# Moving the routing and the scatter of a mixture-of-experts kernel into its recurrence loop, with expert tiles of 256 slots

## The chip, the cores and the metric

The kernel runs on one core of one Trainium2 chip. The metric is device time in microseconds (us). Three runs of the kernel before took 1472.67, 1475.0 and 1470.46 us; the median is 1472.67.

## What is computed

Inputs are x and f_logit (4 sequences of 5056 tokens, 256 wide), a lower bound for the gate, 8 expert embeddings, and two weight matrices for each expert (256x1024 and 1024x256).

```python
sig = 1.0 / (1.0 + np.exp(-f_logit))
f = lower_bound + (1.0 - lower_bound) * sig
i = 1.0 - f
for t in range(S):                      # per sequence, h starts at 0
    h = f[:, t] * h + i[:, t] * x[:, t]
    y[:, t] = h
```

All 4 x 5056 = 20224 rows of y then go through a router and one expert each:

```python
logits = (y / |y|) @ (emb / |emb|).T / tau
expert_idx = argmax(logits)             # one of 8
gate_w = softmax(logits)[expert_idx]
out = gate_w * (relu(y @ w1[expert_idx]) @ w2[expert_idx])
```

## The kernel before

Three stages follow one another, each with its own pools of memory. Every engine's program is written out by hand with its waits on semaphores; there is no scheduler. [...]

**Stage 1, the recurrence** (lines 186 to 400), 79 rounds of 256 tokens. SyncE loads x and f_logit. TensorE transposes both so that the 256 channels lie on partitions (`xT_ps`, `flT_ps`, lines 388 and 398). ScalarE makes the gate (tanh line 327, an affine line 331, and 1 - f line 337). VectorE multiplies (line 254) and runs the recurrence as a scan along the tokens (line 270). TensorE multiplies the result by a matrix that holds both the identity and the 8 expert embeddings (`merged_mms`, line 359); so `psum_rt` has the rows back in token order and, in its first 8 columns, their logits. VectorE copies both out, rows to `Yt_sb` for all 158 blocks of 128 tokens, and ScalarE sums the squares of each row (line 316). Beside this GpSimd fills the scratch table `XsScratch` with null rows (line 161, 166 transfers) and loads all weights as bf16 (lines 165 and 169).

**Stage 2, routing** (lines 460 to 563). All engines wait for stage 1 (`barrier_waits`). VectorE handles all 158 x 8 logits at once: the largest, a one-hot, the gate weight, and with two sets of matmuls (lines 582 and 587) the slot of each token in a table sorted by expert, where each expert's part is padded to a multiple of 128. Then GpSimd scatters the rows, one indirect transfer for each block of 128 tokens (line 558), 158 in all.

**Stage 3, the experts** (lines 565 to 765), 166 blocks of 128 slots. SyncE loads a block from the table (line 610) into one of four buffers `xsb`; from the fifth block on it first waits until the output of the block four places before has landed. TensorE transposes it (line 628), reads the number of its expert into a register (line 635), multiplies by w1 with tokens on the partitions of the result (line 642), transposes the hidden layer of the block before (line 659), and multiplies that of two blocks before by w2 (line 671). ScalarE applies relu (line 743), VectorE copies out both transposes (lines 701 and 708) and scales the output by the gate weight (line 721). GpSimd writes the rows to their places with an indirect transfer (line 750). The wait that closes the ring over the buffers is

```python
if sblk >= 4:
    sp.wait_ge(s_od[sblk % 2], 16 * (sblk // 2 - 1))
sp.dma_start(xsb[r4][:], Xs[sblk * P : (sblk + 1) * P, :])
```

## Time and profile before

| | |
|---|---|
| median of 3 runs | 1472.67 us (1470.46 to 1475.0) |
| profiled execution, its span from first to last instruction | 1469.9 us; no other time is given for it |
| mean granted TensorE clock | 0.820 of full speed |
| busy TensorE matmul / weight load / VectorE / ScalarE / GpSimd | 863.2 / 534.4 / 514.6 / 431.3 / 420.8 us |
| moved by DMA | 104.90 MB |
| share of the chain that ended last | TensorE 30%, DMA 25%, VectorE 12%, "issue" 12%, GpSimd 10%, ScalarE 8% |

The span is the time from the first to the last instruction of one profiled execution; the median of the runs lies 2.8 us above it. PE is TensorE, PEld its weight loads, DVE VectorE, ACT ScalarE, POOL GpSimd, SP SyncE. A wait is put down to what ended it. "Issue" is time in which an engine waited for nothing that the profile shows. [...]

### The profile page before, as it was taken

To read this page: it belongs to the slowest core of one execution; us is meant where nothing else is said; L and a number is where in the kernel's file an instruction comes from. 1 tells how busy PE (TensorE), PEld (TensorE's weight loads), DVE (VectorE), ACT (ScalarE), POOL (GpSimd) and SP (SyncE) were. 2 spreads that over 40 slices of the span, in tenths; PEclk is the share of its full clock that TensorE was granted. 3 is DMA by queue.
4 is the path that set the end of the run, shared out by engine and by line. 5 is a ranking of instruction groups with operands and counts; after the bars stand their busy time and mean duration, and the time that the engine had idled before them with its cause. 6 is when DMAs were issued, how large, how long until landed. Compare 5 with 4: busy or idle time off the path is not lost.

```text
span 1469.9 us, 18961 instructions
## 1 busy us (share of the span) xinstructions
PE 863.2 (59%) x4930; PEld 534.4 (36%) x4930; DVE 514.6 (35%) x1121; ACT 431.3 (29%) x805; POOL 420.8 (29%) x521
## 2 busy tenths in 40 slices
PE   5666676665100000377777777777777777777765
PEld 4555555554000000133434433333443433334433
DVE  4664566666700000123322233323323323233222
ACT  5775677775100000111112121111211111212111
POOL 9890000000077777312121111211111112111121
PEclk9998999999555555589888888988888888888887
DMA  7899844442011111111111111111111111111110
GB/s 214 235 231 235 178 130 129 128 124 64 4 53 53 52 49 53 37 41 39 39 43 39 38 38 41 40 37 43 37 41 39 36 39 41 35 42 39 39 41 20
DMA packets 96104, 104.90 MB, mean 71 GB/s; under 512 B 13828, under 2 KB 83727, under 8 KB 96016
## 3 DMA queue, kind: packets, MB, share of 16 engines
q1 hardware_dynamic: 67184, 52.67, 13.0%
q0 software_dynamic: 28832, 51.03, 12.3%
q8 instruction: 58, 0.95, 0.3%
q14 instruction: 30, 0.25, 0.1%
HBM read 69.42 MB, written 43.66 MB: 77 GB/s over the span
## 4 chain that ended last, share of the span: by engine, by line
PE 30%; DMA 25%; DVE 12%; issue 12%; POOL 10%; ACT 8%; POOLq 0%; DVEq 0%; SPq 0%; ACTq 0%
DMA out_dram<-osb,xsb 14%; DMA xsb<-XsScratch 11%; POOL XsScratch L558 10%; PE psum_h L642 10%; PE psum_o L671 8%; PE psum_rt L359 6%; PE hT_ps L659 4%; ACT fg L331 3%; DVE osb L721 3%; DVE Yf L270 3%; ACT junk L316 2%; PE ysT_ps L628 2%; DVE ixb L254 2%; ACT ig L337 2%; ACT th L327 2%
## 5 line engine op out<-in xcount | busy, mean ns | idle before, releaser
L743 ACT ACTIVATE h_sb<-psum_h 128x1024 bf16<-128x1024 f32 x166 | 169.8, 1023 | 913.9 <-PE psum_h L642 913.9
L750 POOL DMA_INDIRECT out_dram<-osb,xsb x166 | 163.2, 983 | 696.2 <-DVE osb L721 683.2
L628 PE MATMUL ysT_ps<-identb,xsb 128*128 128x128 bf16 x332 | 51.1, 240 | 408.9 <-DMA xsb<-XsScratch 408.4
L671 PE MATMUL psum_o<-w2b,hTt_sb 128*128 x1328 | 272.3, 312 | 0.8
L642 PE MATMUL psum_h<-w1b,ys_sb 128*128 x664 | 232.4, 485 | 60.5 <-DVE ys_sb L701 35.3
L359 PE MATMUL psum_rt<-RHS,Yf 128*128 128x264 f32 x632 | 165.1, 406 | 97.1 <-DVE R L286 93.7
L671 PEld LDWEIGHTS psum_o<-w2b,hTt_sb 128*128 128x128 bf16 x1328 | 149.6, 113 | 152.0 <-issue 68.8
L628 PEld LDWEIGHTS ysT_ps<-identb,xsb 128*128 128x128 bf16 x332 | 23.6, 103 | 438.4 <-issue 236.1
L558 POOL DMA_INDIRECT XsScratch<-Yt_sb,sloti x158 | 152.8, 967 | 88.2 <-issue 50.7
L717 DVE TENSOR_TENSOR gt<-xsb 128x1 f32<-128x1 bf16 x166 | 26.5, 160 | 412.8 <-PE psum_o L671 412.8
L701 DVE COPY ys_sb<-ysT_ps 128x256 bf16<-128x256 bf16 x166 | 47.8, 288 | 346.2 <-PE ysT_ps L628 345.9
L359 PEld LDWEIGHTS psum_rt<-RHS,Yf 128*128 128x128 f32 x632 | 118.1, 197 | 130.0 <-DVE Yf L270 97.2
L642 PEld LDWEIGHTS psum_h<-w1b,ys_sb 128*128 128x128 bf16 x664 | 71.5, 108 | 157.7 <-issue 113.5
L708 DVE COPY hTt_sb<-hT_ps 128x1024 bf16<-128x1024 bf16 x166 | 114.4, 689 | 36.6 <-PE hT_ps L659 36.1
L659 PE MATMUL hT_ps<-identb,h_sb 128*128 128x128 bf16 x1328 | 121.6, 245 | 2.5 <-ACT h_sb L743 2.0
L270 DVE TENSOR_TENSOR_SCAN Yf<-fg,Yf,ixb 128x256 f32<-128x256 f32 (+2 forms) x156 | 107.4, 729 | 2.8
L659 PEld LDWEIGHTS hT_ps<-identb,h_sb 128*128 128x128 bf16 x1328 | 96.9, 111 | 4.8 <-ACT h_sb L743 4.7
L254 DVE TENSOR_TENSOR ixb<-ig,xT_ps 128x512 f32<-128x512 f32 x79 | 54.3, 688 | 125.1 <-ACT ig L337 125.1
L161 POOL DMA_DIRECT2D XsScratch<-fillt x166 | 88.3, 541 | 6.2 <-issue 5.9
L331 ACT ACTIVATE fg<-th,cs 128x256 f32<-128x256 f32 x158 | 86.2, 592 | 2.6
L721 DVE TENSOR_SCALAR osb<-psum_o,gt 128x256 f32<-128x256 f32 x166 | 80.3, 484 | 5.9
L316 ACT ACTIVATE junk<-psum_rt 128x256 f32<-128x256 f32 x158 | 60.6, 383 | 72.1 <-PE psum_rt L359 69.5
(91 smaller groups left out, 448.4 us busy)
## 6 DMA issues: line engine op xcount, KB each, us to landing
xin<-in_x_dram SPq DMA_DIRECT2D x79, 256.0 KB, 2.9
flin<-in_f_logit_dram SPq DMA_DIRECT2D x79, 256.0 KB, 3.2
XsScratch<-fillt POOLq DMA_DIRECT2D x166, 66.0 KB, 4.0
xsb<-XsScratch SPq DMA_DIRECT2D x166, 66.0 KB, 1.8
w1b<-in_moe_w_dram POOLq DMA_DIRECT2D x8, 512.0 KB, 18.0
w2b<-in_moe_w_dram POOLq DMA_DIRECT2D x8, 512.0 KB, 43.1
out_dram<-osb,xsb POOLq DMA_INDIRECT x166, 2.4
XsScratch<-Yt_sb,sloti POOLq DMA_INDIRECT x158, 2.3
```

The source lines that it names most:

```text
L270: ins = v.tensor_tensor_scan(Yf[q][:, dh, 0:first_end], fg[q][:, dh, 0:first_end], ixb[q][:, dh, 0:first_end], init, ALU.mult, ALU.add,)
L331: ins = act.activation(fg[q][:, dh, :], th[q][:, dh, :], AF.Identity, bias=cs[:, dh, 0:1], scale=cs[:, dh, 1:2],)
L359: ins = pe.matmul(psum_rt[:, blk, 0:TCW], Yf[qq][:, dh, blk * P : (blk + 1) * P], RHS[dh][:, :], start=(dh == 0), stop=(dh == DT - 1),)
L558: g.indirect_dma_start(out=Xs[:, :], out_offset=bass.IndirectOffsetOnAxis(ap=sloti[:, j : j + 1], axis=0), in_=Yt_sb[:, j, 0:RWD], in_offs ...
L628: ins = pe.transpose(ysT_ps[:, kt, :], xsb[r4][:, kt * P : (kt + 1) * P], identb[:])
L642: ins = pe.matmul(psum_h[q][:, half * FH : (half + 1) * FH], ys_sb[q][:, kt, :], w1b[:, bass.ds(ev, 1), kt, half * FH : (half + 1) * FH], ...
L659: ins = pe.transpose(hT_ps[:, kf, :], h_sb[q][:, kf * P : (kf + 1) * P], identb[:])
L671: ins = pe.matmul(psum_o[q][:, :], hTt_sb[q][:, kf, :], w2b[:, bass.ds(ev, 1), kf, :], start=(kf == 0), stop=(kf == FT - 1),)
L708: v.tensor_copy(hTt_sb[q][:], hT_ps[:]).then_inc(s_htev, 1)
L721: v.tensor_scalar(osb[q][:], psum_o[q][:], gt[q][:, 0:1], None, op0=ALU.mult).then_inc(s_oev, 1)
L743: act.activation(h_sb[q][:], psum_h[q][:], AF.Relu).then_inc(s_hev, 1)
L750: g.indirect_dma_start(out=out[:, :], out_offset=bass.IndirectOffsetOnAxis(ap=xsb[r4][:, 258:260].bitcast(I32), axis=0), in_=osb[q][:], in ...
```

## The change

It is a new program for the same computation. Operations are recorded one after another with what each depends on (`Prog.op`), and a helper (`resolve`, `emit`) writes each engine's list in the order of recording, with the waits that are still needed. No planner reorders anything.

- **Rounds of 512 tokens**, 40 of them, software-pipelined: round c issues the gate of c+1, the scan of c, the transposes of x for c+1 and of f for c+2, and the transposes back of the output of c-1 (`y_ps`), with eviction (`yev_`) and squares (`sq_`) on ScalarE.
- **Routing by group** of two rounds (1024 tokens; the last two rounds are groups of their own). After the second round of a group: logits and norms by matmuls with 8 and 1 columns of weights (`lg_`), a round later a copy (`lgev_`), transposes (`rt_`), one-hot and running count (`d1_`) and slots by matmul (`psl_`), then gate weight and slot numbers (`d2_`, `d3_`) and 8 scatters. An expert's rows go into a part of the table of its own with room for all tokens, so no count over all tokens is needed first, and no fill. Null rows are scattered behind each expert's last row at the end (16 transfers).
- **Weights** are loaded one matrix every other round instead of at the start.
- **Experts**: 86 tiles of 256 slots; a small table made after the loop gives each tile its first row and its expert, read into registers. w1 is the stationary operand, addressed by register, so that the hidden layer comes out with its channels on partitions and is used by the second matmul as it is. Relu is shared by ScalarE and VectorE. Six load buffers and four output buffers.

The core of the diff:

```diff
+    CH = 512
+    T = 256
+    CAP = N + T
+    NT = N // T + E - 1
...
+        def lg_(g):
...
+                for kt in range(DT):
+                    for k_, c in enumerate(cc):
+                        i = e.matmul(
+                            lg_ps[32 * k_ : 32 * k_ + 8, 0:n], eT[:, kt, :], hb[c % 4][:, kt, 0:n],
...
+                        i = e.matmul(
+                            lg_ps[64 + 32 * k_ : 64 + 32 * k_ + 1, 0:n], onesf[:, 0:1],
+                            sq[c % 3][:, kt, 0:n], start=(kt == 0), stop=(kt == DT - 1),
...
+            lgh[g] = pe(
+                fn, h_eT, h_lgz, h_of, [sqh[c] for c in cc], lgev[g - 1] if g else None
+            )
...
+            rth[g] = pe(fn, lgev[g], r_[g - 1]["slt"] if g else h_eT)
...
+            r["nr2"] = pool(
+                lambda e: e.tensor_tensor(nr2[q][:, 0:J], nrm[q][:, 0:J], half[:, 0:J], ALU.pow),
...
+                    scat[g] = op(
+                        "pool",
+                        lambda e, j=j, b=b, k_=k_: e.indirect_dma_start(
+                            out=Xs[:, :],
...
+        for c in range(NCH + 5):
+            if c + 1 < NCH:
+                gate_(c + 1)
+            if c < NCH:
+                scan_(c)
+            if c + 3 < NCH:
+                load(c + 3)
+            if c + 1 < NCH:
+                X_(c + 1)
+            if c + 2 < NCH:
+                F_(c + 2)
+            if 0 <= c - 1 < NCH:
+                yo_(c - 1)
+                yev_(c - 1)
+                sq_(c - 1)
+                if c - 1 in last_of:
+                    g = last_of[c - 1]
...
+                    lg_(g)
+                    pend.append([c, g, 0])
+            for ent in sorted(pend, key=lambda t: t[1]):
+                while ent[2] < 3 and (c >= NCH - 1 or ent[2] < c - ent[0]):
+                    advance(ent)
...
+            if c % 2 == 0 and wi < 2 * E:
+                wload(wi)
...
+        def xload(j):
+            def fn(e):
+                r = e.value_load(tbl[j : j + 1, 0:1], min_val=0, max_val=NULLROW)
+                return e.dma_start(
+                    xsb[j % NX][:].bitcast(I32), Xs[bass.ds(r, T), :].rearrange("(p s) r -> p s r", s=2)
...
+        def mm1(j):
+            for g in range(4):
+                def fn(e, g=g):
+                    if g == 0:
+                        evr[j] = e.value_load(tbl[j : j + 1, 1:2], min_val=0, max_val=E - 1)
...
+                            i = e.matmul(
+                                ph[g][:, fi * T : (fi + 1) * T],
+                                w1b[:, bass.ds(ev, 1), kt, f * P : (f + 1) * P],
+                                ys[j % 2][:, kt, :],
...
+        def mm2(j):
...
+                        i = e.matmul(
+                            po[s],
+                            hT[j % 2][:, kf, s * P : (s + 1) * P],
+                            w2b[:, bass.ds(ev, 1), kf, :],
...
+        for j in range(NT + 1):
+            if j < NT:
+                mm1(j)
+            if j + 1 < NT:
+                yt_(j + 1)
+            if j >= 1:
+                mm2(j - 1)
```

How the lists of TensorE change at two places. In the loop, before, one round of 256 tokens (`merged_mms` is the last pair):

```order
L388 MATMUL xT_ps<-ident,xin 128x128 [waits s_ix,s_flin0,s_xin0]
L388 MATMUL xT_ps<-ident,xin 128x128 x3
L398 MATMUL flT_ps<-ident,flin 128x128 [waits s_th]
L398 MATMUL flT_ps<-ident,flin 128x128 x3
L359 MATMUL psum_rt<-RHS,Yf 128x264 [waits s_nsq,s_yev,s_yf]
L359 MATMUL psum_rt<-RHS,Yf 128x264 x3
```

In the loop, now, from the end of one round to the routing of the next (`fl_ps` holds f, `y_ps` the output, `lg_ps` the logits, `rt_ps` their transposes and the slots; `s_act` counts ScalarE, `s_dve` VectorE):

```order
L588 MATMUL lg_ps<-sq,onesf 1x512
L492 MATMUL xT_ps<-ident,xin 128x128 [waits s_xin0,s_dve]
L492 MATMUL xT_ps<-ident,xin 128x128 x7
L477 MATMUL fl_ps<-ident,fin 128x128 [waits s_fin1,s_act]
L477 MATMUL fl_ps<-ident,fin 128x128 x7
L558 MATMUL y_ps<-ident,hb 128x128 x8
L631 MATMUL rt_ps<-ident,lgS 128x98 [waits s_act]
L631 MATMUL rt_ps<-ident,lgS 128x98 x3
L697 MATMUL rt_ps<-oh,trib 128x64 [waits s_dve]
L698 MATMUL rt_ps<-offm,onesb 128x64
L703 MATMUL rt_ps<-oh,onesb 128x56
L703 MATMUL rt_ps<-oh,onesb 128x48
```

The matmuls with 264 columns are gone; transposes back, logit matmuls and the routing's small matmuls stand in the list between the transposes of one round and those of the next.

In the expert stage, before (`REGISTER_ALU` and `ISA` work out an address in registers, `TENSOR_LOAD` reads the expert's number):

```order
L659 MATMUL hT_ps<-identb,h_sb 128x128 x7
L635 TENSOR_LOAD EBi
L642 ISA [waits s_hev,s_ysev]
L642 ISA x2
L642 MATMUL psum_h<-w1b,ys_sb 128x512
L642 ISA x2
L642 MATMUL psum_h<-w1b,ys_sb 128x512
L642 ISA x2
L642 MATMUL psum_h<-w1b,ys_sb 128x512
L642 ISA x2
L642 MATMUL psum_h<-w1b,ys_sb 128x512
L671 ISA [waits s_oev,s_htev]
```

And now, at the turn from the second layer of one tile to the first layer of the next but one:

```order
L994 REGISTER_ALU
L994 MATMUL y_ps<-w2b,hT 128x256 x2
L994 REGISTER_ALU
L994 MATMUL y_ps<-w2b,hT 128x256 x2
L960 TENSOR_LOAD tbl [waits s_dve,s_act]
L960 ISA x2
L965 ISA
L965 MATMUL fl_ps<-ys,w1b 128x256
L965 ISA
L965 MATMUL fl_ps<-ys,w1b 128x256
L965 ISA
L965 MATMUL fl_ps<-ys,w1b 128x256
```

One register instruction stands ahead of each matmul of the first layer and of each pair of the second, where there were two for each matmul, and the transposes of the hidden layer are gone.

## Rows read from the trace of the kernel before

**Rows 1.** Busy time by stage: us, engines' busy time (instructions), granted clock, DMA.
```profile
0.00:361.00 361.00, 240.90 (x1266) 195.58 (x1266) 220.89 (x415) 256.25 (x632) 104.53 (x196) 0.98 0.65 170
361.00:605.50 244.50, 6.76 (x12) 3.25 (x12) 33.31 (x42) 5.22 (x8) 153.04 (x159) 0.52 0.13 44
605.50:1470.00 864.50, 615.52 (x3652) 335.56 (x3652) 260.36 (x664) 169.82 (x166) 163.23 (x166) 0.84 0.13 38
```
**Rows 2.** The chain that ended last, 990 to 1020 us, shares by line.
```profile
by line: DMA out_dram<-osb,xsb 24.2%; DMA xsb<-XsScratch 23.3%; PE psum_h L642 15.7%; PE psum_o L671 11.9%; issue 9.5%; PE hT_ps L659 7.2%; PE ysT_ps L628 3.5%; DVE osb L721 3.3%; DVE gt L717 1.1%; POOLq L750 0.3%
```
**Rows 3.** Timeline, GpSimd in stage 2: start, duration, engine, line.
```profile
403.61 0.97 POOL L558 DMA_INDIRECT XsScratch<-Yt_sb,sloti  x1 [0.30 <-issue]
404.88 0.96 POOL L558 DMA_INDIRECT XsScratch<-Yt_sb,sloti  x1 [0.30 <-issue]
```
**Rows 4.** Groups by line and shape: count, busy us, mean ns, idle before.
```profile
L743 ACT ACTIVATE h_sb<-psum_h 128x1024 bf16<-128x1024 f32 x166 | 169.8, 1023 | 913.9 <-PE psum_h L642 913.9
...
L270 DVE TENSOR_TENSOR_SCAN Yf<-fg,Yf,ixb 128x256 f32<-128x256 f32 x150 | 104.5, 739 | 2.7
...
L254 DVE TENSOR_TENSOR ixb<-ig,xT_ps 128x512 f32<-128x512 f32 x79 | 54.3, 688 | 125.1 <-ACT ig L337 125.1
...
L327 ACT ACTIVATE th<-flT_ps 128x512 f32<-128x512 f32 x79 | 47.1, 597 | 18.9 <-PE flT_ps L398 18.8
```
**Rows 5.** Short windows, TensorE alone: us, busy (instructions), granted clock, DMA.
```profile
116.50:117.00 0.50, 0.00 (x0) 1.00 1.12 236
118.50:119.00 0.50, 0.50 (x3) 0.50 1.07 229
121.00:121.50 0.50, 0.50 (x2) 0.50 1.09 227
122.00:122.50 0.50, 0.50 (x4) 1.00 1.10 236
```
**Rows 6.** Timeline, TensorE, the same stretch.
```profile
118.49 1.08 PE L388 MATMUL xT_ps<-ident,xin 128*128 128x128 f32 x4 [2.33 <-issue]
119.37 1.06 PE L398 MATMUL flT_ps<-ident,flin 128*128 128x128 f32 x4
```
**Rows 7.** Timeline, VectorE in the routing.
```profile
384.13 0.17 DVE L506 TENSOR_SCALAR PAD<-PAD 128x8 f32<-128x8 f32 x1
384.34 0.17 DVE L507 TENSOR_SCALAR PAD<-PAD 128x8 f32<-128x8 f32 x1
```
**Rows 8.** Timeline, first weight load of the loop, and a later round.
```profile
8.09 0.71 PEld L388 LDWEIGHTS xT_ps<-ident,xin 128*128 128x128 f32 x4 [1.89 <-DVE RHS L242]
...
252.77 0.60 PE L388 MATMUL xT_ps<-ident,xin 128*128 128x128 f32 x4
...
253.21 0.60 PE L398 MATMUL flT_ps<-ident,flin 128*128 128x128 f32 x4
...
253.90 0.60 ACT L327 ACTIVATE th<-flT_ps 128x512 f32<-128x512 f32 x1
```
**Rows 9.** Timeline, weight loads of matmuls with 512 f32 columns.
```profile
371.20 0.19 PEld L587 LDWEIGHTS ps_b<-OH,onesm 128*128 128x128 f32 x1 [0.24 <-issue]
371.63 0.19 PEld L587 LDWEIGHTS ps_b<-OH,onesm 128*128 128x128 f32 x1 [0.24 <-issue]
```
**Rows 10.** DMA issues: queue, count, us to landing.
```profile
out_dram<-osb,xsb POOLq DMA_INDIRECT x166, 2.4
```
**Rows 11.** Timeline, expert stage: weight loads, and a copy that releases one.
```profile
1008.99 0.85 PEld L671 LDWEIGHTS psum_o<-w2b,hTt_sb 128*128 128x128 bf16 x7 [0.28 <-issue]
...
1010.31 0.45 PEld L659 LDWEIGHTS hT_ps<-identb,h_sb 128*128 128x128 bf16 x8 [0.24 <-ACT h_sb L743]
...
1010.77 0.28 DVE L701 COPY ys_sb<-ysT_ps 128x256 bf16<-128x256 bf16 x1
...
1011.47 0.73 PEld L642 LDWEIGHTS psum_h<-w1b,ys_sb 128*128 128x128 bf16 x4 [0.71 <-issue]
...
1012.37 1.52 PEld L671 LDWEIGHTS psum_o<-w2b,hTt_sb 128*128 128x128 bf16 x8 [0.18 <-issue]
```

## The prediction

> **What bounds the kernel now.** I read the busy table by stage first [rows 1]. The reader is to see three stages that do not overlap: 361 us in which the recurrence runs and TensorE is busy for 241; 244.5 us in which TensorE does 6.8 us of work and GpSimd 153; and 864.5 us of expert layers, in which no engine is busy for more than 72%. So no engine bounds the kernel; what bounds it differs by stage, and the sum has to be made by stage.

> In the expert stage the chain of waits [rows 2] is a ring: almost half of it is two transfers, the scatter of a block's output (24.2%) and the load of the block four places later (23.3%), since that load waits until the output that uses the same buffer has landed. TensorE stands idle meanwhile; 166 blocks share 864.5 us, 5.2 us each. In the middle stage the scatters into the scratch table are issued one by one: from one to the next is 1.27 us [rows 3], and 158 of them make 201 of the 244.5 us. The rest is the routing arithmetic over all tokens. In the first stage, 79 rounds of 256 tokens, nothing but the first transfer ahead is waited for long; 361 / 79 is 4.6 us a round, or 18.3 us for 1024 tokens.

> **The loop after the change.** One routing group is 1024 tokens, two rounds of 512. GpSimd then issues 8 scatters in a group, 8 x 1.27 = 10.2 us, about 11.5 with one weight load and three small operations; whether that hides depends on the length of a group. The order of TensorE's queue says what the length is: in the odd round the tile transposes `rt` wait for ScalarE's copy of the logits and the slot matmuls wait for VectorE's one-hot, and the next round's transposes stand behind both; in the even round the logit matmuls wait for ScalarE's squares. So a group is a chain that hops between engines, and I price the chain:
> - Odd round. Eviction of the recurrence's output and its squares, each 128x1024: 1.02 us each by the 128x1024 activation [rows 4]; the copy of the logits (98x512) by the 128x512 one, 0.60. Together 2.64.
> - `rt`, 4 transposes. TensorE has then waited for 2.6 us. [...] I take the lower level here: 1.08 us for four [rows 6].
> - VectorE: seven operations on 64 elements until the one-hot, two more for the carry, then the gated input `nx` on which the next transposes wait. Small operations start 0.21 us apart [rows 7], 9 x 0.21 = 1.9; `nx` is 128x1024 where the row is 128x512 at 0.688 [rows 4]. Doubling with a fixed part of 0.155 gives 1.22. The slot matmuls run beside it.
> - 24 transposes (x, f, output): four take 0.44 from start to start at the upper level [rows 8] and 0.88 at the lower [rows 6]. Half at each: 3.96.
> - Even round. Eviction and squares again, 2.04. Then 8 logit matmuls of 512 f32 columns. The only such rows, at the upper level, are loaded 0.43 us apart [rows 9]: 3.44. Then 24 transposes at the upper level, 2.64, and 0.75 for half a chance that this round also starts at the lower level (3 us at half speed lose 1.5).
> - Ten handoffs between engines; from the end of a transpose to the tanh that waits for it is 0.09 [rows 8]: 0.9.

> Sum 2.64 + 1.08 + 1.9 + 1.22 + 3.96 + 2.04 + 3.44 + 2.64 + 0.75 + 0.9 = 20.6 us a group, which is longer than the 18.3 that these tokens cost now. Under it lie GpSimd's 11.5; VectorE's two `nx`, four scans of 512 (0.739 for 256 [rows 4], 1.3 each) and 15 small operations, about 11; ScalarE's about 10. The middle stage so disappears into the loop, and the loop gets slower. If that cover went, GpSimd's 11.5 us a group would be the next limit and not the scatters' full 201 us. Traffic does not bind: 0.65 of 361 us is 235 us of all DMA engines [rows 1]; the fill of the table, 166 issues, leaves it and the scatters, 0.13 of 244.5 us, come in.

> 19.75 groups x 20.6 = 407. Ahead of it 10 us: the first transposes start at 8.1 today [rows 8], and here they stand behind two larger loads. Behind it 20 us: the last tokens run through the chain with nothing beside them (about 13), 21 small operations make the tile table (4.4), the last scatters and the first load land (2.4 by the output scatter's row [rows 10], in part beside the table). The expert layers start at 437 instead of 605.5.

> **The expert layers after the change.** There are 86 tiles of 256 slots whatever the counts, and a tile issues 4 transposes, 16 matmuls of 256 columns with register-addressed weights, 16 with a register-addressed moving side. The 8 transposes of the middle layer and their eviction go. Loads use six buffers: a tile's output lands about 5 us (two issues and 2.4) after it is evicted, while five tiles are still to come, so the ring of [rows 2] opens and TensorE should run back to back. Its rate is then set by its queue. Eight output matmuls started 0.20 apart where the queue had just been empty (8 loads in 1.52 us [rows 11]); there, two register instructions stood ahead of each. Where the queue had been full, seven loads took 0.85, 0.12 apart. Transposes without registers are loaded 0.056 apart. I read a register instruction as about 0.075 and a matmul with its load as 0.05 of issue. Now one stands ahead of each of the first 16 (0.13 each, 2.1) and half of one ahead of the others (0.11, 1.75). Transposes 0.25. The expert's number is read into a register once a tile: in [rows 11] the copy ends at 1011.05 and the matmuls behind three register instructions start at 1011.47; I take 0.4 for this. 4.5 us a tile, 86 x 4.5 = 387. VectorE has at most 2.8 us a tile (two 128x512, a copy and an output, none above the 0.69 of a 128x512 [rows 4]), ScalarE two at 0.60 and an output, under 1.8, GpSimd 2 x 1.27; all hidden. The last tile's eviction, two issues and landing add 5. Padded null rows: 16 scatters, 20 us, are issued beside the first tiles, whose outputs queue behind them; four output buffers cover that.

> [...]

> **Sum.** 437 + 387 + 5 = 829 for the profiled span, against 1469.9 now. The runs' median stands 3 us above that span; forecast 832.

> Ends of the unknown prices: with TensorE at the upper level throughout, a group loses 1.32, 0.75 and 0.48: 18.1, and the total 782. At the lower level throughout it is 27.2: 963. A tile at 4.1 or 5.2 moves the total by -34 or +60.

> **The rivals.**
> - The logit matmuls overlap. Each group of four writes other output partitions (0, 64, 32, 96) with 8 or 1 columns of weights. If four run together, 8 take two slots, 0.86 instead of 3.44, 2.58 a group, 51 us: 781. No row here shows narrow matmuls, so nothing speaks for it or against it but that f32 matmuls one after another took 0.43. Chance 0.2. [...]
> - Registers bind. If it is not the register instructions but the register-addressed matmul itself that costs 0.20, a tile is 32 x 0.20 + 0.65 = 7.05: 219 us more, 1051. For it: 0.20 was seen only on such matmuls. Against: 0.12 was seen on them too. Chance 0.12, the load rule above included.
> - The clock stays low in the loop because of the waits: 963, as above. For it: every long wait of [rows 5] was followed by 0.50. Against: it came back each time under work. Chance 0.1.
> - The scatters are not hidden: if they wait, on their queue, behind the weight loads until the loop's end, 158 x 1.27 = 201 us stay outside and the total is 1030. Against: 11.5 of 20.6 us. Chance 0.04.
> - Slower than before. If each register-addressed matmul must wait until its address is there and then until its weights are, the 0.42 us between release and start in [rows 11] would be paid 32 times a tile: 14.1 us, 826 us more, 1658. It decides from 0.35 us a matmul on. Against: eight such matmuls in 1.52 us. Chance 0.01.

> **How the numbers follow.** Forecast 0.5 (832, itself between 798 and 892 by the two prices of a tile); overlap 0.2; registers 0.12; low clock 0.1; scatters 0.04; slower 0.01; the remaining 0.03 lies below 740. From 740 to 960 leaves out registers, scatters, slower, half of the low clock: about 0.2. Within 0.3% (4 us, about what a measurement of this kernel can tell from no change) there is no case: 0.005; slower by more 0.01; faster by more 0.985.

> **What would show it.** The stage table: expert layers start near 437, and no stretch between has GpSimd alone. In the loop, TensorE's waits on ScalarE and VectorE are its largest, a group takes about 20.6 us, with granted clock well under 1. In the expert stage TensorE waits for no load, the clock is 1.00, and a tile takes 4.5 us. If the expert stage takes over 450, the register price is wrong; if a group takes under 18, the logits overlap or the clock held; if GpSimd's scatters run on after the loop for over 30 us, the hiding failed.

## The result, and the profile after

The changed kernel took 821.54 us (median of 4 runs, 817.68 to 822.01) beside 1472.78 us of the kernel before, measured together: ratio 0.5577, 95% interval 0.5559 to 0.5594. The forecast was 832. The profiled execution spans 819.3 us, the mean granted clock is 0.856, DMA moved 95.02 MB. Measured once more, later, the same kernel took 799.66 us (798.65 to 800.45; ratio 0.5440, 0.5414 to 0.5466). The experiments are compared with that second measurement (`again`) where nothing else is said, and what lies between the two is told below.

The table by stage answers to [rows 1]; columns are us, then busy time (instructions) of TensorE, its weight loads, VectorE, ScalarE, GpSimd, then granted clock, DMA share, GB/s.

```profile
0.00:424.50 424.50, 240.35 (x1553) 175.76 (x1553) 201.11 (x473) 190.80 (x245) 232.49 (x282) 0.76 0.54 144
424.50:805.00 380.50, 362.82 (x3074) 278.89 (x3075) 188.35 (x342) 140.85 (x256) 177.14 (x181) 0.97 0.28 89
805.00:819.30 14.30, 2.82 (x25) 2.07 (x22) 0.97 (x2) 0.95 (x2) 4.39 (x5) 0.75 0.01 0
```

Three stages became two; the third row is only the end of the second, in which the last output lands. In the first, no engine is busy for more than 57% of the time; in the second TensorE is for 95% until that end, at a clock of 0.97 where [rows 1] had 0.84. The expert stage fell from 864.5 to 394.8 us, 470 less; what stands ahead of it fell from 605.5 to 424.5, 181 less. The waits by engine and line (us in total, times, longest) say what the loop consists of:

```profile
ACT Yt L571 <- PE y_ps L558: 168.7, 36, 6.6
POOL XsScratch L777 <- DVE Yt L759: 100.1, 18, 8.0
PE lg_ps L584 <- ACT sq L548: 57.6, 20, 18.5
PE rt_ps L631 <- ACT lgS L602: 30.9, 13, 3.0
DVE rs L730 <- POOL nr L685: 18.9, 3, 17.0
```

GpSimd waits in the loop, so its scatters are hidden, as forecast; TensorE waits for ScalarE, as forecast. One group in the timeline (start, duration, what, idle before and its releaser), TensorE's rows and those it waits for:

```profile
203.80 0.60 PE L584 MATMUL lg_ps<-hb,eT 128*8 128x512 f32 x1 [2.06 <-ACT sq L548]
203.81 0.59 PE L588 MATMUL lg_ps<-sq,onesf 128*1 128x512 f32 x1
203.82 0.60 PE L584 MATMUL lg_ps<-hb,eT 128*8 128x512 f32 x1
203.82 0.59 PE L588 MATMUL lg_ps<-sq,onesf 128*1 128x512 f32 x1
...
206.68 1.68 PE L492 MATMUL xT_ps<-ident,xin 128*128 128x128 f32 x8
...
210.14 1.02 ACT L571 ACTIVATE Yt<-y_ps 128x1024 bf16<-128x1024 f32 x1 [3.78 <-PE y_ps L558]
211.06 1.05 ACT L548 ACTIVATE sq<-hb 128x1024 f32<-128x1024 f32 x1
212.01 0.59 ACT L602 ACTIVATE lgS<-lg_ps 98x512 f32<-98x512 f32 x1
...
212.65 0.56 PE L631 MATMUL rt_ps<-ident,lgS 98*128 98x98 f32 x4 [2.55 <-ACT sq L548]
...
214.92 1.21 DVE L520 SCALAR_TENSOR_TENSOR nx<-fg,xT_ps 128x1024 f32<-128x1024 f32 x1
...
216.19 1.97 PE L492 MATMUL xT_ps<-ident,xin 128*128 128x128 f32 x8 [1.16 <-issue]
...
221.61 1.02 ACT L571 ACTIVATE Yt<-y_ps 128x1024 bf16<-128x1024 f32 x1 [6.54 <-PE y_ps L558]
...
223.63 0.60 PE L584 MATMUL lg_ps<-hb,eT 128*8 128x512 f32 x1 [2.06 <-ACT sq L548]
```

The hops stand in the order in which the forecast priced them. This group takes 223.63 - 203.80 = 19.83 us; the mean over 17 groups, from one copy of the logits (`lgS`) to the next, is 19.27. Group times below are such means. The clock in the same stretch, TensorE's busy time alone:

```profile
204.50:207.50 3.00, 3.00 (x16) 0.50 0.56 195
208.00:214.50 6.50, 2.66 (x24) 1.00 0.67 217
215.00:221.50 6.50, 5.34 (x25) 0.50 0.36 57
```

So after the waits between 210.1 and 216.2 all 24 transposes of the odd round had a granted clock of 0.50, and the later half of the logit matmuls had it after the wait that ends at 203.8. What the two levels cost shows on rows of eight transposes: at 1.00 the next row starts 0.88 us later (208.19 to 209.07, the first of them 1.04 long, so rows overlap), at 0.50 1.71 later (217.95 to 219.66, 1.91 long). Costs of matmuls are such distances from start to start; upper and lower level below mean 1.00 and 0.50. In the expert stage a tile runs without a wait, 4.18 us here, 4.23 on average:

```profile
600.63 0.39 PE L940 MATMUL lg_ps<-identb,xsb 128*128 128x128 bf16 x4
600.85 1.91 PE L994 MATMUL y_ps<-w2b,hT 128*128 x16
602.75 1.20 PE L965 MATMUL fl_ps<-ys,w1b 128*128 128x256 bf16 x8
603.78 1.19 PE L965 MATMUL xT_ps<-ys,w1b 128*128 128x256 bf16 x8
604.81 0.39 PE L940 MATMUL rt_ps<-identb,xsb 128*128 128x128 bf16 x4
```

Only the first tiles show something that no row of before announced:

```profile
441.51 0.69 DVE L985 TENSOR_SCALAR hT<-xT_ps 128x512 bf16<-128x512 f32 x1 [11.94 <-remote]
...
444.29 1.89 PE L965 MATMUL fl_ps<-ys,w1b 128*128 128x256 bf16 x8 [13.46 <-DVE ys L950]
```

"Remote" means a releaser that the profile cannot name. The matmuls whose results VectorE copies here had ended by 430.9.

### The profile page after: what moved, and what is told of

Read it like the earlier page. It is cut to its first block, busy times and chain, and to the rows that moved or that the text cites. A ratio compares the mean times of both kernels' runs of the same rounds, so it can differ in the third digit from the quotient of the medians.

```text
span 819.3 us, 14640 instructions
## 1 busy us (share of the span) xinstructions
PE 606.0 (74%) x4649; PEld 456.7 (56%) x4649; DVE 390.4 (48%) x817; ACT 332.6 (41%) x503; POOL 414.0 (51%) x466
## 2 busy tenths in 40 slices
DMA packets 78868, 95.02 MB, mean 116 GB/s; under 512 B 9217, under 2 KB 68877, under 8 KB 78800
## 4 chain that ended last, share of the span: by engine, by line
PE 70%; issue 10%; ACT 7%; DVE 6%; POOL 3%; another core or an unknown queue 2%; DMA 1%; SPq 0%; POOLq 0%; DVEq 0%; ACTq 0%
PE y_ps L994 18%; PE fl_ps L965 12%; PE xT_ps L965 11%; PE xT_ps L492 7%; PE fl_ps L477 6%; PE y_ps L558 6%; PE lg_ps L584 5%; ACT sq L548 3%; ACT Yt L571 3%; POOL XsScratch L777 2%; DVE nx L520 2%; PE lg_ps L940 1%; PE rt_ps L940 1%; PE rt_ps L631 1%
## 5 line engine op out<-in xcount | busy, mean ns | idle before, releaser
L777 POOL DMA_INDIRECT XsScratch<-Yt,sli x158 | 155.1, 981 | 144.5 <-DVE Yt L759 100.1
L994 PE MATMUL y_ps<-w2b,hT 128*128 x1376 | 165.3, 274 | 0.9 <-DVE osb L1012 0.9
L994 PEld LDWEIGHTS y_ps<-w2b,hT 128*128 128x128 bf16 x1376 | 131.4, 98 | 15.4 <-issue 1.1
L965 PE MATMUL fl_ps<-ys,w1b 128*128 128x256 bf16 x688 | 104.1, 284 | 17.1 <-DVE ys L950 14.9
L965 PE MATMUL xT_ps<-ys,w1b 128*128 128x256 bf16 x688 | 103.6, 283 | 0.2 <-issue 0.2
L965 PEld LDWEIGHTS fl_ps<-ys,w1b 128*128 x688 | 66.3, 96 | 60.8 <-issue 40.6
L584 PE MATMUL lg_ps<-hb,eT 128*8 128x512 f32 (+1 forms) x160 | 54.8, 784 | 57.6 <-ACT sq L548 57.6
L538 DVE TENSOR_TENSOR_SCAN hb<-fg,hb,nx 128x512 f32<-128x512 f32 (+4 forms) x78 | 93.5, 1238 | 1.4
L492 PE MATMUL xT_ps<-ident,xin 128*128 128x128 f32 x316 | 67.0, 381 | 22.8 <-DVE nx L520 16.3
L965 PEld LDWEIGHTS xT_ps<-ys,w1b 128*128 x688 | 66.5, 97 | 25.2 <-issue 1.6
L510 ACT ACTIVATE fg<-th,cs 128x512 f32<-128x512 f32 (+1 forms) x80 | 60.3, 801 | 1.3
```

What stands on the lines that cost most here:

```text
L492: i = e.transpose(xT_ps[:, dh, b * P : (b + 1) * P], xin[q][:, b, dh * P : (dh + 1) * P], ident[:],)
L510: lambda e, dh=dh: e.activation(fg[q][:, dh, 0:n], th[q][:, dh, 0:n], AF.Identity, bias=cs[:, dh, 0:1], scale=cs[:, dh, 1:2],),
L538: lambda e, dh=dh, s0=s0, s1=s1, init=init: e.tensor_tensor_scan(hb[c % 4][:, dh, s0:s1], fg[q][:, dh, s0:s1], nx[q][:, dh, s0:s1], init, ...
L584: i = e.matmul(lg_ps[32 * k_ : 32 * k_ + 8, 0:n], eT[:, kt, :], hb[c % 4][:, kt, 0:n], start=(kt == 0), stop=(kt == DT - 1),)
L777: lambda e, j=j, b=b, k_=k_: e.indirect_dma_start(out=Xs[:, :], out_offset=bass.IndirectOffsetOnAxis(ap=sli[g % 4][:, j : j + 1], axis=0), ...
L965: i = e.matmul(ph[g][:, fi * T : (fi + 1) * T], w1b[:, bass.ds(ev, 1), kt, f * P : (f + 1) * P], ys[j % 2][:, kt, :], start=(kt == 0), sto ...
```

## The experiments

The loop rests on two claims (TensorE's waits are a chain of hops; the waits also cost clock), the logit matmuls on a price that the trace puts in doubt, the expert stage on the ring and on registers. The runs take these in turn. `serial`, `swap`, `fill` and `static` ran on another chip than `again`; `serial`, whose change did nothing, has a mean group of 18.91 us there against 18.85 in `again`, so the chip hardly shifts what is compared.

**Logit matmuls in another order** (`serial`): the loops over accumulation steps and column groups change places.

```diff
-for kt in range(DT):
-    for k_, c in enumerate(cc):
+for k_, c in enumerate(cc):
+    for kt in range(DT):
         i = e.matmul(
             lg_ps[32 * k_ : 32 * k_ + 8, 0:n], eT[:, kt, :], hb[c % 4][:, kt, 0:n],
...
+for k_, c in enumerate(cc):
+    for kt in range(DT):
         i = e.matmul(
             lg_ps[64 + 32 * k_ : 64 + 32 * k_ + 1, 0:n], onesf[:, 0:1],
```

> The eight logit and norm matmuls of a group are the same, but follow one another by output partition group (all of group 0, then 32, 64, 96) instead of in turn. Theory: the four groups run side by side only because neighbours in the queue go to different column groups. Then 4 slots of 0.43 us become 13 (the last of one group overlaps the first of the next): 9 x 0.43 = 3.9 us more in each of 19 full groups, more where the clock is low: 895 to 920 us. Rival: they overlap because the weights are narrow (8 or 1 columns), whatever the order: 821 +- 3 us.

802.29 us (800.55 to 803.75). Against the 799.66 of the unchanged order that is 0.3% more, with the group time nearly the same, so which matmuls are neighbours does not matter:

```profile
220.82 0.61 PE L584 MATMUL lg_ps<-hb,eT 128*8 128x512 f32 x2 [2.06 <-ACT sq L548]
220.86 0.60 PE L590 MATMUL lg_ps<-sq,onesf 128*1 128x512 f32 x2
221.26 0.60 PE L584 MATMUL lg_ps<-hb,eT 128*8 128x512 f32 x2
```

The norm matmuls (L590) stand behind all logit matmuls (L584) of the group in the queue, and start 0.04 us after the first of them. By column group is meant the block of 32 output partitions that a matmul writes to: 0, 32, 64 and 96 on here. Whether the column groups are the reason stayed open, hence:

**All in one column group** (`onegroup`), in the order of `serial`.

```diff
-lg_ps[32 * k_ : 32 * k_ + 8, 0:n]
+lg_ps[0:8, 0:n]
-lg_ps[64 + 32 * k_ : 64 + 32 * k_ + 1, 0:n]
+lg_ps[0:1, 0:n]
```

> All logit and norm matmuls of a group write the same output partitions, from 0 on, one accumulation after another (so norms and logits of the even rounds overwrite each other and the routing is another; the rows that the later steps read elsewhere stay zero). Theory: matmuls with few columns of weights run side by side when their outputs lie in different groups of 32 partitions, whatever their order in the queue; in one group all 16 records of 0.43 us follow one another, 6.9 us instead of 1.7: 5.2 us a group at the upper clock, 10 at the lower, 100 to 190 us more than the 800 of the changed kernel: 890 to 990 us. Rival: narrow weights are enough, 795 to 810.

894.44 us (894.00 to 894.89), 94.8 more; the mean group is 23.87 us against 18.85 in `again`.

```profile
199.12 3.60 PE L584 MATMUL lg_ps<-hb,eT 128*8 128x512 f32 x8 [2.06 <-ACT sq L548]
202.55 3.60 PE L590 MATMUL lg_ps<-sq,onesf 128*1 128x512 f32 x8
206.08 1.10 PE L492 MATMUL xT_ps<-ident,xin 128*128 128x128 f32 x8
```

7.0 us for the set, one after another, where four at a time took 1.7 to 2.9. Narrow weights alone are not enough; the separate outputs are worth 5 us a group. In `onegroup` the matmuls also write the same addresses one after another; one column group with separate addresses was not tried, so the addresses as the cause are not excluded.

**Squares ahead of the eviction** (`swap`).

```diff
+sq_(c - 1)
 yo_(c - 1)
 yev_(c - 1)
-sq_(c - 1)
```

> In each round ScalarE squares the scan's output before it evicts the transposes of that output, instead of after; the logit matmuls need the squares alone. Theory: a group is a chain of hops, and eviction plus squares (2.0 us in the even round, 0.95 of it in the odd one) stand on it: the logit matmuls start as soon as the transposes end, a group falls from 19.8 by 2 to 3 us, the run by 40 to 60: 760 to 780 us. Rival: another engine's own work (VectorE or GpSimd) is just behind and takes the wait over: 810 to 821 us.

765.63 us (761.90 to 769.08), 34 less than the unchanged kernel; a group falls from 18.85 to 17.13. That is 1.7 of the 2 to 3 us, because the rival came true in part. The wait, and one first scatter of a group:

```profile
DVE rs L730 <- POOL nr L685: 97.9, 19, 16.6
```
```profile
201.34 1.05 POOL L777 DMA_INDIRECT XsScratch<-Yt,sli  x1 [3.37 <-DVE Yt L759]
```

GpSimd's square root `nr` of a group stands behind the eight scatters of the group before. With a group of 19 us that cost 0.5 us or nothing; at 17 VectorE waits up to 5.35 us for it, and the next `nx`, which TensorE needs, stands behind. So does VectorE's `Yt`, the gate weight for which the next scatters wait: the two engines wait for each other in a ring of 17 us (4.4 from `rs` to the end of `Yt`, 0.3 to the scatter, 10.2 for eight scatters, 2.0 for the square root with the add and multiply behind it).

**Fillers in the waits** (`fill`): 27 matmuls a group that nobody reads (bf16, 512 columns), in TensorE's three waits: 9 ahead of the logit matmuls, 10 ahead of the transposes of the logits, 8 behind the slot matmuls. In the trace of the run eight take 1.72 us (280.28 to the next row's start at 282.00), 0.215 each, so 27 are 5.8 us.

```diff
...
+for _ in range(k):
+    i = e.matmul(
+        t[:].rearrange("p (b c) -> p b c", b=4), identb[:],
+        identb[:].unsqueeze(1).to_broadcast([P, 4, P]), start=True, stop=True,
+    )
...
```

> [...] Theory: the waits cost twice, once as such and once because the clock is at 0.50 after them; with the waits filled the granted clock of the loop is near 1.00, the 24 transposes of the odd round take 2.7 instead of 5.4 us and the logit matmuls 1.7 instead of 2.9, about 4 us a group less, minus up to 1.5 by which fillers end late: 745 to 775 us. Rival: the clock falls for another reason, and the fillers, at 0.43 us each, only delay: 840 to 900 us.

766.74 us (765.25 to 769.29), 33 less although TensorE does more. The stretch from 40 to 360 us, the unchanged kernel (`again`) first and then with fillers:

```profile
40.00:360.00 320.00, 199.58 (x1316) 151.54 (x1317) 165.74 (x362) 159.59 (x204) 190.85 (x200) 0.77 0.60 153
```
```profile
40.00:360.00 320.00, 270.86 (x1934) 162.31 (x1934) 177.50 (x407) 167.80 (x214) 203.82 (x218) 0.98 0.58 156
```

The waits lowered the clock, and that cost 1.8 us a group (18.85 to 17.07) where 2.5 to 4 were expected; then the same wait as in `swap` appears (`rs` on `nr`, 76.5 us in 18 times). Two different cures end at 17.1 us because the same ring is next.

**The hops off TensorE's list** (`hoist`): each piece of the routing gets its own place in a round (`st1` to `st3` are the groups whose last round lies 2, 3 and 4 rounds back; `d1_` holds GpSimd's square root, `d3_` the scatters). "The run before" below is `swap`.

```diff
     gate_(c + 1)
+for g in st1:
+    lgev_(g)
...
     X_(c + 1)
+for g in st2:
+    d2_(g)
+for g in st1:
+    rt_(g)
...
     F_(c + 2)
+    sq_(c - 1)
+for g in st1:
+    d1_(g)
...
     yo_(c - 1)
     yev_(c - 1)
-    sq_(c - 1)
+for g in st1:
+    psl_(g)
...
         lg_(g)
+for g in st3:
+    d3_(g)
```

> Squares ahead of the eviction as in the run before; besides, the copy of the logits, their transposes and the one-hot of a group come earlier in the odd round (before the transposes back and the eviction of that round), the slot matmuls behind those, and GpSimd's square root stands ahead of the scatters of the group before instead of behind them. Theory: with the squares moved, VectorE waited 5.35 us a group for that square root behind eight scatters, and TensorE 1.6 + 1.35 + 1.06 us for the copy, the one-hot and nx; all four go, and a group (17 us there, 19.2 before) comes to GpSimd's or VectorE's own work, 12 to 14 us: 690 to 725 us. Rival: each hop taken off TensorE's queue comes back on VectorE's, which then holds the scan up: 745 to 765.

713.35 us (712.22 to 716.55); a group takes 14.11 us. GpSimd's rows, one group:

```profile
204.68 1.22 POOL L777 DMA_INDIRECT XsScratch<-Yt,sli  x1 [0.30 <-issue]
205.89 0.96 POOL L456 DMA_DIRECT2D w2b<-in_moe_w_dram  x1
206.88 1.68 POOL L681 TENSOR_TENSOR nr<-nrm,half 128x8 f32<-128x8 f32 x1
...
208.92 0.15 POOL L766 IOTA Yt<- 128x8 int32 x1
209.88 1.09 POOL L777 DMA_INDIRECT XsScratch<-Yt,sli  x1 [0.81 <-DVE df L740]
```

From scatter to scatter it works without a wait on others (the profile names VectorE's `df`, which had ended 0.53 us before): the "next limit" of the prediction, 11.5 us there, is reached and is 14, since the square root takes 1.7 and not a small operation's time and the first scatter starts 0.8 us behind the token numbers (`IOTA`). Several places were changed at once here, so what each is worth is not shown.

**Trimming GpSimd** (`tight`, on top of `hoist`): the token numbers one round earlier, `nr3`, the add and multiply behind the square root, on VectorE.

> The kernel with the hoisted routing; GpSimd writes the token numbers of a group one round earlier, so that its scatters no longer wait 0.80 us for that, and the add and multiply behind its square root (0.19) go to VectorE. Theory: GpSimd is now the bound of the loop (a group of 14.2 us is 8 scatters of 1.27, 1.7 to 2.1 for the square root, the wait of 0.80, a weight load of 0.8 to 0.96): 1.0 to 1.1 us a group less over 20 groups, 20 us: 690 to 698 us. Rival: TensorE's waits still bind and GpSimd only looks full: 708 to 714.

706.75 us (704.82 to 707.90), 6.6 less instead of 20, and a group of 13.97 us. The wait for the token numbers went, but another of 0.86 us came in its place:

```profile
215.96 1.69 POOL L688 TENSOR_TENSOR nr<-nrm,half 128x8 f32<-128x8 f32 x1
217.69 0.17 DVE L692 TENSOR_SCALAR nr<-nr 128x8 f32<-128x8 f32 x1 [1.29 <-POOL nr L688]
218.03 0.20 DVE L766 RECIPROCAL Yt<-den 128x8 f32<-128x8 f32 x1
218.52 1.05 POOL L777 DMA_INDIRECT XsScratch<-Yt,sli  x1 [0.86 <-DVE Yt L766]
```

The moved operation stands in VectorE's list ahead of `Yt`, and waits for the square root; the scatter waits for `Yt` and starts 0.29 us after its end, as in 18 of 19 groups (0.28 to 0.30). In `hoist`, `Yt` was done 5 to 7 us before most first scatters. So one half of the edit gave back what the other saved, and GpSimd stays the limit; neither the range nor the rival (708 to 714) was met. Token numbers moved alone were not tried. This is the fastest kernel of the study, 0.4796 of before (0.4768 to 0.4824).

**The ring alone** (`bring`): the kernel before with eight load and four output buffers.

```diff
...
-r4, k4 = sblk % 4, sblk // 4
-if sblk >= 4:
-    sp.wait_ge(s_od[sblk % 2], 16 * (sblk // 2 - 1))
+r4, k4 = sblk % 8, sblk // 8
+if sblk >= 8:
+    sp.wait_ge(s_od[sblk % 4], 16 * (sblk // 4 - 1))
...
```

> The kernel before with eight load buffers and four output buffers in the expert stage instead of four and two, and nothing else. Theory: the ring of output scatter and load bound that stage (47% of the chain); opened, a block costs what TensorE, busy 72% of the stage, needs: 3.5 to 4 us instead of 5.2, 200 to 280 us less: 1190 to 1270 us. Then half or more of what the changed kernel gains in its expert stage (484 us) is due to the buffers alone. Rival: the chain of evictions from block to block is just as long, and the waits only change their name: 1400 to 1470.

1287.44 us (1285.68 to 1288.42; ratio 0.8752, 0.8710 to 0.8794): 185 us less, just short of the range.

```profile
607.50:1286.00 678.50, 526.34 (x3596) 289.15 (x3652) 239.18 (x664) 169.83 (x166) 163.21 (x166) 0.99 0.16 48
```

The stage falls from 864.5 to 678.5 us and its clock rises from 0.84 [rows 1] to 0.99. So in the kernel before the buffers alone are worth 186 of the 470 us that the expert stage gained (864.5 to 394.8; the 484 in the expectation leaves out the last 14 us); the rest came with the new tile. The split holds in this order only: the new tile with too few buffers gains nothing, as the next run shows.

**Three and four load buffers** in the changed kernel (`ring3`, `ring4`: `NX = 3`, `NX = 4`).

> The changed kernel with three load buffers for the expert tiles instead of six. From the transposes of a tile to its last output matmul pass 10.8 us, then an eviction of 0.5, two scatter issues, a landing and a load, about 8 us: a buffer is held 18.8 us. Theory: this ring sets the rate as soon as buffers x 4.18 us is less: with three 6.3 us a tile, 86 x 2.1 = 180 us more: 960 to 1020 us, and TensorE's transposes wait for the load. With six (25 us) it does not bind, and its opening is why the tile is TensorE's own. Rival: loads are not what a tile waits for, 805 to 830.

1436.33 us (1433.66 to 1439.01): the ring binds, but at 11.8 us a tile, nearly twice the count.

```profile
602.85 3.57 PE L994 MATMUL y_ps<-w2b,hT 128*128 x16
...
609.01 0.98 POOL L1019 DMA_INDIRECT out_dram<-osb,xsb  x1 [0.30 <-issue]
612.20 0.34 SPq L926 DMA_DIRECT2D xsb<-XsScratch  x1
614.29 0.61 PE L940 MATMUL lg_ps<-identb,xsb 128*128 128x128 bf16 x4 [6.13 <-DMA xsb<-XsScratch]
614.69 3.62 PE L994 MATMUL y_ps<-w2b,hT 128*128 x16
```

The transposes of a later tile stand ahead of the second matmuls in TensorE's list, and wait for a load that waits for the output of the tile just before.

> The changed kernel with four load buffers instead of six. Three gave 11.8 us a tile where 6.3 was expected. Theory formed from that trace: the transposes of tile j+2 stand ahead of tile j's second matmuls in TensorE's list, so with three buffers the ring (second matmuls 3.5 at the low clock, eviction 0.5, wait and two issues 3.2, landing 2.4, load 2.1, transposes 0.4) closes over one tile, and with n buffers over n - 2. Four buffers: 10.2 (second matmuls at the upper clock) to 11.8 over two tiles, 5.1 to 5.9 us a tile, 84 x 0.9 to 1.7 more than the 800 us of the changed kernel: 875 to 945 us. Rival, the count that failed with three (18.8 us held, shared by the buffers): 4.7 a tile, 835 to 845.

922.46 us (917.84 to 927.07). Some of that is stalls without a releaser in the loop and at the first tiles (33.3 us on ScalarE and 11.3 on VectorE in its trace), so the tiles decide: two took 11.0 us (transposes at 601.53 and 612.52), 5.5 each, and the mean tile is 5.3, inside the new theory's 5.1 to 5.9 and not the old one's 4.7. With three and four buffers the ring closes over n - 2 tiles; by the same count six leave four tiles, 16.9 us, for a ring of 10 to 12.

**Fixed weight addresses** (`static`): `bass.ds(ev, 1)` becomes `j % E`.

> The expert's number is not read into a register: tile j uses the weights of expert j mod 8 at fixed addresses (so most tiles are multiplied by other weights than the reference's). Theory: registers cost a gap of 0.26 to 0.3 us a tile and 0.025 for each of the 16 first matmuls: 4.18 becomes 3.5 to 3.6 us a tile, 86 x 0.6 = 52 us less: 765 to 775. Rival 1: 0.13 a matmul is the rate of 256 columns with their weight load, and only the gap goes: 795 to 800. Rival 2: PE hides both, 821.

752.60 us (752.00 to 753.66), 47 less than the unchanged kernel, below the range of the theory (765 to 775), which was counted from the first measurement; a tile takes 3.72 us instead of 4.23, where 3.5 to 3.6 was expected. From start to next start, the 16 matmuls of the second layer now take 1.75 us and eight of the first layer 0.87:

```profile
601.47 1.91 PE L990 MATMUL y_ps<-w2b,hT 128*128 128x256 bf16 x16
603.22 1.04 PE L962 MATMUL fl_ps<-ys,w1b 128*128 128x256 bf16 x8
604.09 1.04 PE L962 MATMUL xT_ps<-ys,w1b 128*128 128x256 bf16 x8
```

**The register a tile ahead** (`tightev`). "The run before" below is `tight`.

> The run before, and the register with the next tile's expert is read between the first and second quarter of a tile's first matmuls, a tile ahead. Theory: the gap of 0.26 us ahead of a tile's first matmuls is the read of the register alone; the fixed addresses saved 0.48 us a tile, 0.26 of it by the gap: 86 x 0.26 = 22 us less than the run before. Rival 1: the read stalls TensorE's queue wherever it stands, and the gap only moves: within 3 us of the run before. Rival 2: 40 us less, if the slower pace of the addressed matmuls (0.13 against 0.109) comes from an emptied queue too.

710.68 us (709.89 to 711.93): 3.9 us more than `tight`, nearest to the first rival (within 3). The gap, 0.26 us ahead of the first quarter in `tight`, moved to the new place of the read, ahead of the second quarter, and is longer there (0.62 in this row, 0.36 and 0.42 in the next two tiles):

```profile
560.88 0.47 PEld L959 LDWEIGHTS fl_ps<-ys,w1b 128*128 x4 [0.62 <-issue]
```

**Once more, unchanged** (`again`).

> The changed kernel as it is, beside the other runs of this call. Its trace had two stretches in which engines stood still with no releaser that the profile can name: 5.4 us on ScalarE ahead of an eviction in the loop, and 11.9 us on VectorE at the first expert tile, on which TensorE waited 13.5 us. The run with the logit matmuls in another order had neither and was 19 us shorter, with the same group time. Theory: the two stalls belong to the build or the place of the code, not to the change, and may be absent here: 800 to 805 us. Rival: they come with this order of instructions each time: 818 to 823.

799.66 us. Neither of the two stalls without a releaser is there. Of the variants only `ring4` had such stalls (33.3 us in six on ScalarE's eviction in the loop, 11.3 on VectorE at the first tile). The expert stage starts at 416.1 instead of 424.9, and from its first transposes to the second tile's matmuls pass 7.3 us instead of 19.4: 8.8 and 12.1 of the 22 us between the two profiled spans (819.3 and 796.9). What caused them stays open: the program is the same. The runs without such stalls ran on two chips and `ring4` on a third; on which the first measurement ran is not on record, so the chip as the cause is neither shown nor excluded.

## Why the prediction was right

- **The sum.** Expert layers from 424.9 (forecast 437), end 819.3 (829). Of the loop's 12 us: groups 19.75 x (20.6 - 19.27) = -26, ahead +1 (first transposes at 11.0), behind the loop about 33 instead of 20: after the last rounds GpSimd still had 16 scatters of two groups and the square root of the next behind them (VectorE waited 17.0 us once, above), then 6 more scatters. "The last scatters in part beside the table" was mis-sized. The expert layers' 394 us against 392 (387 + 5) is luck: the tiles took 86 x 0.27 = 23 us less, the row of tiles took some 12 us more to fill and empty than the 5 counted, and the stall at the first tiles added 12 that `again` does not have. Without the stalls the forecast of 832 would have stood 32 us above the result, 799.66.
- **The chain of hops** is the mechanism: `swap` and `hoist` shorten it and the loop follows, until GpSimd's queue is next. Term by term in the group shown: eviction, squares and copy 2.46 (2.64); `rt` 0.56, at the upper level after 2.55 us without work (1.08 at the lower); VectorE 1.68 (1.9) and `nx` 1.27 (1.22; its fixed part of 0.155 is an estimate that the trace of before supports: 0.688 us for 128x512 at L254 and 1.474 for 128x1264 at L520 leave 0.153); the odd round's transposes 5.42, all at the lower level (3.96); even round 2.02 (2.04); logit matmuls 2.88 (3.44); 24 transposes 3.46 (2.64 + 0.75). Handoffs are nearly all inside these spans: 0.08 us of the 19.83 lie outside (0.9 forecast). That the sum came near is in part luck, since the odd round's transposes cost 1.5 more and the logits, `rt` and handoffs 1.9 less.
- **The logit matmuls** are the step whose price was wrong twice. The trace of before holds two weight loads for one matmul with 512 f32 columns (six records for the three that the code issues, at L582 and at L587; [rows 9] has two of them), so 0.43 us is half a matmul; and four run together (starts at 203.80 to 203.82). One after another they would have cost 6.9, as `onegroup` shows (7.0); together they cost 1.7 at the upper level. The rival on overlap happened, but its time of 781 did not, because the two errors cancel. What the separate outputs are worth is what `onegroup` lost without them, 5.0 us a group.
- **The low clock** lies between forecast (half of a round) and rival (all of it): 0.77 in the loop. It cost at least 1.8 us a group, up to where the next wait took over (`fill`).
- **The ring** opened as forecast: no load wait after the first tile. "While five tiles are still to come" was a wrong count that did not matter: by `ring3` and `ring4` the slack is four tiles.
- **The tile**: 4.23 against 4.5. First layer 2.06 (2.1); second layer with the register gap 1.90 to 2.05 (1.75 + 0.4); transposes 0.22 (0.25). Registers cost 0.51 us a tile (`static`): 0.32 in the first layer (2.06 against 1.74), the rest in the gap, which the one other placement tried did not remove. So a register instruction costs a matmul 0.02 us, not 0.075, and the 256-column matmul with its load of 128 rows takes 0.109 without one (`static`), not 0.05. That the sums of both layers fit is luck; by the forecast's own prices a matmul of the second layer would be 0.09, not the 0.11 that it took. The rival in which addressed matmuls need 0.20 does not hold.
- **Scatters hidden**: right for the loop; the scatters of the last rounds are the part of the drain named above, and only `hoist` comes to GpSimd's own time.

## What to carry to other kernels

When two cures of different waits give the same time, look for the queue that both run into: here a small operation queued on GpSimd behind eight scatters. Before moving an operation to an engine that is less busy, see what stands behind it there: in `tight` it held up the value that the unloaded engine needs next. Count a ring of buffers by the instruction that waits for the load and by what stands behind it on its engine, not by the time a buffer is held. Before a row prices a new instruction, check how many records the trace keeps for one of them.
